# Two blocks of the first layer by turns, eight chunks ahead of them, and stores by block

## Chip, cores and metric

One core of one Trainium2 chip runs the whole program. The metric is device time in microseconds (us), the median of several runs. A profile of one further execution gives the span from its first to its last instruction and what every engine did in it. Five engines work beside each other, each through its own queue in the order in which the program was written down: PE (TensorE, the matmuls), DVE (VectorE), ACT (ScalarE), POOL (GpSimd) and SP, which here only issues DMAs.

## What is computed

A linear attention with a decay per channel, and then two feed-forward layers over 3072 tokens:

```python
batch, n_heads, seq, head_dim = (4, 8, 768, 48)     # d_model 384
for t in range(S):
    state = alpha[:, :, t, :, None] * state + np.einsum('bhd,bhe->bhde', k[:, :, t], v[:, :, t])
    y[:, :, t] = np.einsum('bhd,bhde->bhe', q[:, :, t], state)
x = y as (3072, 384)
h = x @ w_in                    # 384 x 2048
x = (h * np.cos(h)) @ w_out     # 2048 x 384
g, val = x @ w_gate, x @ w_val  # 384 x 1536 each
out = (g / (1 + np.exp(-g)) * val) @ w_out2
```

The weights come as 64-bit floats. Inputs and outputs of the matmuls of the two layers are split into a high and a low part, so that a product takes three matmuls (high by high, low by high, high by low).

## The kernel before

**Chunks.** The attention is cut into 24 chunks: 6 blocks of time (128 steps each) by 4 batches. A chunk loads its q, k and decay table (`attn_load`, `qka`, 112 partitions by 2052 floats) and its v (128 by 576), and `attn` writes down its operations. DVE scans the decays (L392), takes reciprocals (L396) and scans again (L399). POOL multiplies q and k by the results (L393, L402). PE forms the scores (L409), DVE masks them into `sm` (L420, twice), PE transposes k (L431), forms the outputs of the four pairs of heads (L447 from the state, L451 from the scores) and the growth of the state (L439). ACT and DVE then copy the outputs into the high and low part `xh` and `xl` of the block (L467, L471): one instruction for the first three pairs and three for the last pair, whose 96 rows must be spread over partitions 96 to 127 of three columns. DVE adds to the state (L483), POOL fades it (L488). ACT squares two inputs for a range statistic (L494).

**Blocks and slots.** Four chunks make a block of 512 tokens. The first layer takes 16 slots for a block. In a slot (`first_slot`), PE computes 128 hidden channels (`hidden`, L514, nine matmuls of 512 columns into one bank), a chain of ACT and DVE computes h cos(h) (L560, L561, L564, L565, L568, all of which read the bank or `s`), ACT and POOL split it (L526, L527), and PE contracts it into the three sum banks (`contract`, L542 six matmuls, L548 three). Contractions run up to three slots behind (`LAG`). The sum banks are banks 0 to 2. The banks for the hidden channels go round: 6 and 7 in block 0, 5 to 7 from block 1, 3 to 7 in the last block. After a block `spill` scales the sums and stores them. The second layer has 12 slots for a block of 27 matmuls each.

**Weights.** A unit holds one slot's `w_in` and `w_out`. `decode` turns a unit from 64-bit floats into two 32-bit parts: ACT takes the low bits (L278), DVE the upper bits in two halves of 384 columns through bank 5 (L85, L89), POOL adds (L94), ACT and DVE write the high and low part (L295, L300). Units 0 and 1 are decoded among the first chunks, 2 and 3 next, and each other one four slots ahead of its slot in block 0. The later blocks use the same decoded weights. The second layer's 18 units are decoded in blocks 1 to 4 (`stash`, L314 to L323), kept in memory and loaded again (`recall`).

**Order.** `register` writes down all operations with a priority; `Plan.lay` lays them out by a list of costs and priorities, and the engines' queues get that order once and for all. Its first part, before the change: chunks 0 to 3; then block 0, slot by slot, with a decode in each of the first twelve and chunks 4 to 7 spread over the block; then block 1 with chunks 8 to 11, and so on. The planner's numbers set the order alone; at run time each instruction waits for its semaphores.

**The end.** `ending` runs the last contractions bank by bank. A bank's halves are copied by ACT (L646) and DVE (L647), both into one buffer, and stored. `put` (L625) stores a block's result as 128 partitions by 4 batches by 128 columns.

## Time and profile before

| | |
|---|---|
| runs | 1024.91, 1025.81, 1027.52 us; median 1025.81 |
| profiled execution | 1021.61 us, its span 1019.8 us |
| PE busy | 988.0 us (97% of the span) |
| DVE, ACT, POOL busy | 524.8, 506.6, 418.4 us |
| first 150 us: PE, DVE busy | 125.5, 136.2 us |
| 150 to 450 us: PE, DVE busy | 300.0, 234.4 us |

A busy PE is not a PE at its peak, since the ends of matmuls are modelled and neighbours overlap. What it got done in a stretch is read better from the count of its instructions. A matmul of 32-bit attention operands counts as two instructions.

### The profile page before, as it was taken

The numbers are of one execution on the slowest core, as the hardware profiler recorded it, in microseconds if no ns is written. First come the engines' busy times: TensorE is split into PE (matmuls) and PEld (weight loads), VectorE is DVE, ScalarE is ACT, GpSimd is POOL, SyncE is SP. The second block draws the span as 40 slices with busy tenths as digits, with TensorE's granted clock in tenths as the row PEclk, the third lists the DMA queues.
The fourth block names the chain that finished last, engine by engine and source line by source line (L and its number), as shares of the span: only waits on it lengthen the run. The fifth ranks groups of instructions, "written<-read, shape, count | busy, mean of one in ns | idle before, by whom it ended". The sixth has DMA issues, their size and how long they took to land.

```text
span 1019.8 us, 12904 instructions
## 1 busy us (share of the span) xinstructions
PE 988.0 (97%) x4902; PEld 810.3 (79%) x4902; DVE 524.8 (51%) x785; ACT 506.6 (50%) x924; POOL 418.4 (41%) x323
## 2 busy tenths in 40 slices
PE   7689899999999999999999999999999999999997
PEld 7567678888888888888888888888888888888885
DVE  7999997887786788674433222322222222222221
ACT  3487676777777778776767223312212212221211
POOL 5666764555555458453434223223223223222221
PEclk9799999999999999999999999999999999999999
DMA  9456436434463654554576413201101100100101
GB/s 297 147 148 184 143 80 192 123 119 141 136 196 106 178 168 136 151 183 149 187 254 230 171 36 123 91 0 32 31 1 31 31 1 1 31 1 1 31 1 34
DMA packets 33685, 109.54 MB, mean 107 GB/s; under 512 B 2960, under 2 KB 12304, under 8 KB 31440
## 3 DMA queue, kind: packets, MB, share of 16 engines
q1 hardware_dynamic: 33616, 108.64, 35.0%
q8 instruction: 40, 0.66, 0.3%
q14 instruction: 29, 0.24, 0.1%
HBM read 85.04 MB, written 23.59 MB: 107 GB/s over the span
## 4 chain that ended last, share of the span: by engine, by line
PE 90%; DVE 7%; DMA 1%; issue 1%; ACT 1%; POOL 0%; DVEq 0%; SPq 0%
PE bank L514 47%; PE bank L542 22%; PE bank L548 11%; PE bank L451 4%; PE bank L409 2%; PE bank L447 2%; PE bank L439 1%; DMA qka<-qka 1%; DVE bank L85 1%; DVE ws L89 1%; DVE qka L399 1%; PE bank L431 1%; DVE pair L300 1%; DVE xl L471 1%; DVE s L568 1%
## 5 line engine op out<-in xcount | busy, mean ns | idle before, releaser
L527 POOL TENSOR_TENSOR glo<-s,ghi 128x512 fp32r<-128x512 f32 x168 | 233.9, 1392 | 483.3 <-ACT ghi L526 447.4
L514 PE MATMUL bank<-xh,late 128*128 128x512 f32 x864 | 282.3, 394 | 0.0
L514 PE MATMUL bank<-xh,pair 128*128 128x512 f32 x576 | 198.8, 400 | 9.1 <-DVE s L568 6.8
L578 DVE TENSOR_TENSOR s<-s,bank 128x512 f32<-128x512 f32 x72 | 49.5, 687 | 281.4 <-ACT s L577 281.4
L514 PEld LDWEIGHTS bank<-xh,late 128*128 128x128 f32 x864 | 162.7, 188 | 37.8
L526 ACT CAST ghi<-s 128x512 fp32r<-128x512 f32 x168 | 103.8, 618 | 160.4 <-DVE s L579 141.1
L514 PE MATMUL bank<-xl,late 128*128 128x512 f32 x432 | 170.1, 394 | 0.0
L542 PE MATMUL bank<-ghi,pair 128*128 128x512 f32 x576 | 151.4, 398 | 0.0
L577 ACT ACTIVATE s<-bank 128x512 f32<-128x512 f32 x72 | 43.1, 598 | 194.0 <-PE bank L514 193.8
L514 PEld LDWEIGHTS bank<-xh,pair 128*128 128x128 f32 x576 | 108.7, 189 | 37.6 <-DVE s L568 9.2
L542 PEld LDWEIGHTS bank<-ghi,pair 128*128 128x128 f32 x576 | 106.9, 188 | 24.9
L514 PE MATMUL bank<-xl,pair 128*128 128x512 f32 x288 | 114.2, 397 | 1.6 <-DVE xl L471 1.6
L542 PE MATMUL bank<-ghi,late 128*128 128x512 f32 x432 | 112.2, 395 | 0.0
L514 PEld LDWEIGHTS bank<-xl,late 128*128 128x128 f32 x432 | 81.4, 188 | 18.9
L542 PEld LDWEIGHTS bank<-ghi,late 128*128 128x128 f32 x432 | 81.3, 188 | 19.0
L561 DVE SCALAR_TENSOR_TENSOR s<-s,bank 128x512 f32<-128x512 f32 x96 | 65.4, 682 | 56.4 <-ACT s L560 55.7
L560 ACT ACTIVATE s<-bank,magic 128x512 f32<-128x512 f32 x96 | 66.0, 688 | 57.2 <-PE bank L514 55.5
L568 DVE SCALAR_TENSOR_TENSOR s<-s,bank 128x512 f32<-128x512 f32 x96 | 65.0, 677 | 45.6 <-ACT s L565 45.2
L548 PE MATMUL bank<-glo,pair 128*128 128x512 f32 x288 | 83.8, 399 | 0.1
L94 POOL TENSOR_TENSOR ws<-ws 128x768 int32<-128x768 int32 x34 | 66.9, 1966 | 40.1 <-DVE ws L89 32.6
L564 ACT ACTIVATE s<-s 128x512 f32<-128x512 f32 x96 | 60.5, 631 | 28.7 <-DVE s L561 28.4
L579 DVE TENSOR_TENSOR s<-s,bank 128x512 f32<-128x512 f32 x72 | 49.5, 687 | 48.3 <-PE bank L514 48.2
(96 smaller groups left out, 1202.7 us busy)
## 6 DMA issues: line engine op xcount, KB each, us to landing
big<-w SPq DMA_DIRECT2D x34, 768.0 KB, 5.5
qka<-qka SPq DMA_DIRECT2D x36, 384.8 KB, 6.3
w2d<-big SPq DMA_DIRECT2D x18, 768.0 KB, 4.1
late<-w2d SPq DMA_DIRECT2D x18, 768.0 KB, 4.3
ws<-w SPq DMA_DIRECT2D x16, 768.0 KB, 4.6
v<-vv SPq DMA_DIRECT2D x22, 288.0 KB, 3.0
x2d<-big SPq DMA_DIRECT2D x6, 768.0 KB, 3.8
big<-x2d SPq DMA_DIRECT2D x6, 768.0 KB, 4.9
```

What stands on the lines that cost most here:

```text
L94: nc.gpsimd.tensor_tensor(a, a, low, ALU.add)
L514: nc.tensor.matmul(h, lhsT=self.part(key, wpart, c), rhs=act[:, c, :], start=(n == 0), stop=(n == 3 * KM - 1))
L526: self.add(ACT, 0.62, prio, lambda: nc.scalar.copy(hi, s), reads=[sc], writes=[hic])
L527: self.add(POOL, 1.29, prio, lambda: nc.gpsimd.tensor_sub(lo, s, hi.bitcast(F32)), reads=[sc, hic], writes=[loc], lock=True)
L542: nc.tensor.matmul(self.banks[m][0], lhsT=self.part(key, wpart, m), rhs=hi, start=(f == 0 and wpart == 0), stop=False)
L548: nc.tensor.matmul(self.banks[m][0], lhsT=self.part(key, 0, m), rhs=lo, start=False, stop=last)
L560: add(ACT, WIDE, p, lambda: nc.scalar.activation(s, h, AF.Identity, bias=self.magic), reads=[hc], writes=[sc])
L561: add(DVE, WIDE, p, lambda: nc.vector.scalar_tensor_tensor(s, s, MAGIC, h, ALU.subtract, ALU.subtract), reads=[hc], writes=[sc])
L564: nc.scalar.activation(s, s, AF.Sin, scale=HALF_TURN)
L568: add(DVE, WIDE, p, lambda: nc.vector.scalar_tensor_tensor(s, s, 0.5, h, ALU.subtract, ALU.mult), reads=[hc], writes=[sc])
L578: add(DVE, WIDE, p, lambda: nc.vector.tensor_tensor(s, s, hg, ALU.mult), reads=[gc], writes=[sc])
L579: add(DVE, WIDE, p, lambda: nc.vector.tensor_tensor(s, s, hv, ALU.mult), reads=[vc], writes=[sc])
```

## The change

The eight chunks of blocks 0 and 1 are written down first (`for ch in range(2 * B)`), with units 0 to 3 decoded among them. Then the slots of blocks 0 and 1 go by turns: slots 0 to 4 of block 0, then one slot of block 1 after every second slot of block 0, until block 0 is done; then block 1's other ten slots, with chunks 8 to 11 among them; then blocks 2 to 5 as before. Block 0 keeps its sums in banks 0 to 2, every other block has them in banks 3 to 5 (`LATE = 3`). The hidden banks are 6 and 7 until block 0 is done, then 2, 6 and 7, and 0, 1, 2, 6 and 7 from the last block.

In the first eight chunks (`PACKED = 8`) PE writes the last pair's outputs itself to partitions 96 to 127 (`thirds`), so that ACT and DVE each copy all outputs by one instruction. From unit 5 on (`QUICK = 5`) DVE decodes the upper bits in SBUF over all 768 columns at once (two instructions) in place of four halves through bank 5. Chunks 0 to 3 load their inputs in four pieces. Their first state is a product on DVE alone, without POOL's fade. Chunks 4 to 7 take the four input buffers in turn, as 0 to 3 did. The second layer's units are decoded from position 33 on. The result is stored block by block, contiguous in the columns of a block (the host puts the columns in order), and in the ending DVE copies its half of the last bank into a buffer of its own. Most of the planner's costs and priorities have new numbers.

```diff
+PACKED = 8
+QUICK = 5
+LATE = 3
+JOIN = 4
+PACE = 2
+STASH = 33
...
+        if i < QUICK:
+            bits, bc = self.banks[5]
...
+        else:
+            add(DVE, 0.55, prio, lambda: decode_quick(nc, high, a), reads=[rc], writes=[ac], lock=True)
+            add(DVE, 0.95, prio, lambda: decode_sign(nc, high, a, a), reads=[rc], writes=[ac], lock=True)
...
+        if ch < PIECES:
+            for n, p in zip("FRqk", PARTS):
+                self.add(SP, 0.45, prio + p, lambda n=n: piece(n), writes=[cells[n]], lat=0.75)
...
-        base = 0 if ch < FAST and ch % 2 else 3
+        base = 3 if ch < 2 * B and ch % 2 == 0 else 0
...
+        def thirds():
+
+            for j in range(3):
+                part = slice(32 * j, 32 * j + 32)
+                uses = [
+                    (v[:, 3, i : i + 2, :].rearrange("s a e -> s (a e)")[:, part], self.sm[i][0][:, 3, :])
+                    for i in range(2) if j != 2 - 2 * i
+                ]
+                if not first:
+                    uses.insert(0, (st[0:ROWS, 3].rearrange("p a e -> p (a e)")[:, part], q[:, 3, :]))
+                for n, (w, x) in enumerate(uses):
+                    nc.tensor.matmul(o[96:128, j, :], lhsT=w, rhs=x, start=(n == 0), stop=(n == len(uses) - 1))
...
+        if packed:
+            outs = [(o[:, 0:3, :], (slice(0, 128), slice(0, 3), cs))]
...
+                    if first:
+                        nc.vector.tensor_tensor(s, u, fend[lo:hi].unsqueeze(2).to_broadcast([hi - lo, PAIRS, D]), ALU.mult)
...
-            src, c = self.banks[m]
+            src, c = self.banks[y + m]
...
-            outv[:, m, :, blk * C : (blk + 1) * C], ob[:, m, :].rearrange("p (b t) -> p b t", b=B)
+            self.out[m * 128 : (m + 1) * 128, blk * N + cols.start : blk * N + cols.stop], src
...
+            add(ACT, 0.4, prio, lambda m=m, src=src: nc.scalar.copy(ob[:, m, left], src[:, left]), reads=[bc], writes=[own])
+            add(DVE, 0.4, prio, lambda src=src: nc.vector.tensor_copy(other[:, left], src[:, right]), reads=[bc], writes=[oc])
...
+        for ch in range(2 * B):
+            self.attn_load(ch, LOADS[ch])
+            if ch in (1, 2, 3, 4):
+                self.decode(ch - 1, DEC[ch - 1], DLOAD[ch - 1])
+            self.attn(ch, FIRST[ch])
+        order, n1 = [], 0
+        for f in range(F1):
+            order.append((0, f))
+            if f >= JOIN and (f - JOIN) % PACE == 0:
+                order.append((1, n1))
+                n1 += 1
+        order += [(1, f) for f in range(n1, F1)] + [(blk, f) for blk in range(2, NB) for f in range(F1)]
```

PE's queue in the middle of block 0, before. `xh_62` and `xl_63` are block 0's input, banks 104 and 105 are hidden banks 6 and 7, banks 98 to 100 are block 0's sums, and `qka` and `st_88` belong to chunk 4, whose parts stand between the slots:

```order
L514 MATMUL bank_104<-xh_62,pair 128x512
L542 MATMUL bank_98<-ghi_69,pair 128x512 x2
L542 MATMUL bank_99<-ghi_69,pair 128x512 x2
L542 MATMUL bank_100<-ghi_69,pair 128x512 x2
L548 MATMUL bank_98<-glo_73,pair 128x512
L548 MATMUL bank_99<-glo_73,pair 128x512
L548 MATMUL bank_100<-glo_73,pair 128x512
L431 MATMUL bank_101<-ident,qka 128x112 x4
L542 MATMUL bank_98<-ghi_70,pair 128x512 x2
L542 MATMUL bank_99<-ghi_70,pair 128x512 x2
L542 MATMUL bank_100<-ghi_70,pair 128x512 x2
L447 MATMUL bank_102<-qka,st_88 96x128
```

The same engine now, in the middle of block 0 after all eight chunks. `xh_64` and `xl_65` are block 1's input, banks 101 to 103 its sums:

```order
L611 MATMUL bank_99<-glo_73,pair 128x512
L611 MATMUL bank_100<-glo_73,pair 128x512
L576 MATMUL bank_104<-xh_64,pair 128x512
L576 MATMUL bank_104<-xl_65,pair 128x512
L576 MATMUL bank_104<-xh_64,pair 128x512 x2
L576 MATMUL bank_104<-xl_65,pair 128x512
L576 MATMUL bank_104<-xh_64,pair 128x512 x2
L576 MATMUL bank_104<-xl_65,pair 128x512
L576 MATMUL bank_104<-xh_64,pair 128x512
L604 MATMUL bank_101<-ghi_70,pair 128x512 x2
L604 MATMUL bank_102<-ghi_70,pair 128x512 x2
L604 MATMUL bank_103<-ghi_70,pair 128x512 x2
```

No part of a chunk stands between slots there any more; a slot of block 1 takes the place, by weights that are decoded already.

DVE's queue in block 0, before. Two steps of a slot's chain (L561, L568) hold four halves of a decode between them; `big` is the raw unit, bank 103 is bank 5:

```order
L561 SCALAR_TENSOR_TENSOR s_66<-s_66,bank_105 128x512
L85 TENSOR_SCALAR bank_103<-big_77 128x384
L89 SCALAR_TENSOR_TENSOR ws<-big_77,bank_103 128x384
L85 TENSOR_SCALAR bank_103<-big_77 128x384
L89 SCALAR_TENSOR_TENSOR ws<-big_77,bank_103 128x384
L568 SCALAR_TENSOR_TENSOR s_66<-s_66,bank_105 128x512
L561 SCALAR_TENSOR_TENSOR s_67<-s_67,bank_104 128x512
L85 TENSOR_SCALAR bank_103<-big_78 128x384
L89 SCALAR_TENSOR_TENSOR ws<-big_78,bank_103 128x384
L85 TENSOR_SCALAR bank_103<-big_78 128x384
L89 SCALAR_TENSOR_TENSOR ws<-big_78,bank_103 128x384
L568 SCALAR_TENSOR_TENSOR s_67<-s_67,bank_104 128x512
```

The same engine now, in the part where blocks 0 and 1 go by turns (L627 and L634 are the chain's steps, L103, L107 and L325 the decode's):

```order
L627 SCALAR_TENSOR_TENSOR s_67<-s_67,bank_105 128x512
L103 TENSOR_SCALAR ws<-big_78 128x768
L107 SCALAR_TENSOR_TENSOR ws<-big_78,ws 128x768
L325 TENSOR_TENSOR pair<-ws,pair 128x768
L634 SCALAR_TENSOR_TENSOR s_67<-s_67,bank_105 128x512
L627 SCALAR_TENSOR_TENSOR s_68<-s_68,bank_104 128x512
L103 TENSOR_SCALAR ws<-big_77 128x768
L107 SCALAR_TENSOR_TENSOR ws<-big_77,ws 128x768
L634 SCALAR_TENSOR_TENSOR s_68<-s_68,bank_104 128x512
L627 SCALAR_TENSOR_TENSOR s_66<-s_66,bank_105 128x512
L325 TENSOR_TENSOR pair<-ws,pair 128x768
L634 SCALAR_TENSOR_TENSOR s_66<-s_66,bank_105 128x512
```

A decode's upper bits are two instructions there, both from SBUF to SBUF, and of three slots in a row one has no decode of upper bits in its chain.

## Rows read from the trace of the kernel before

**Rows 1.** Stretches: from:to, length, busy us (count) of each engine, PEclk, DMA.

```profile
0.00:150.00 150.00, 125.49 (x768) 105.29 (x769) 136.18 (x215) 97.43 (x188) 95.07 (x82) 0.94 0.58 168
6.00:49.00 43.00, 29.32 (x223) 26.88 (x222) 39.99 (x61) 18.59 (x47) 24.80 (x20) 0.84 0.76 237
49.00:150.00 101.00, 91.55 (x527) 73.77 (x526) 95.52 (x150) 77.36 (x139) 66.46 (x48) 0.98 0.50 137
150.00:450.00 300.00, 300.00 (x1679) 248.64 (x1678) 234.43 (x333) 221.96 (x417) 171.06 (x126) 1.00 0.52 151
600.00:1000.00 400.00, 400.00 (x1725) 324.27 (x1724) 95.70 (x146) 96.73 (x164) 97.33 (x76) 1.00 0.09 28
```

**Rows 2.** Stretches, PE and PEld alone: L514 (two rows), then L542, then L548.

```profile
0.00:150.00 150.00, 41.04 (x153) 28.35 (x153) 0.94 0.58 168
150.00:450.00 300.00, 127.24 (x504) 94.07 (x504) 1.00 0.52 151
...
0.00:150.00 150.00, 20.96 (x80) 14.99 (x81) 0.94 0.58 168
...
0.00:150.00 150.00, 11.41 (x39) 7.13 (x39) 0.94 0.58 168
```

**Rows 3.** Waits of PE, 45 to 120 us: in total, times, longest.

```profile
PE bank L514 <- DVE s L568: 6.0, 5, 2.7
```

**Rows 4.** Timeline, DVE's first scan: start, us, operation, idle before it.

```profile
6.37 1.23 DVE L392 TENSOR_TENSOR_SCAN qka<-qka,starts 112x516 f32<-112x516 f32 x1 [4.81 <-DMA qka<-qka]
```

**Rows 5.** DVE's groups by line, 6 to 49 us: count, busy us, mean ns, idle before.

```profile
L399 DVE TENSOR_TENSOR_SCAN qka<-qka,rb 112x512 f32<-112x512 f32 x3 | 5.9, 1958 | 0.1
L471 DVE SCALAR_TENSOR_TENSOR xl<-bank,xh 32x128 fp32r<-32x128 f32 (+1 forms) x16 | 5.6, 351 | 1.0 <-ACT xh L467 0.8
L420 DVE COPY_PREDICATED sm<-mask,bank 128x512 f32<-128x512 int32 x8 | 5.4, 726 | 0.3 <-PE bank L409 0.2
L392 DVE TENSOR_TENSOR_SCAN qka<-qka,starts 112x516 f32<-112x516 f32 x3 | 4.4, 1463 | 5.4 <-DMA qka<-qka 5.3
...
L85 DVE TENSOR_SCALAR bank<-big 128x384 int32<-128x384 int32 x6 | 3.3, 558 | 0.1
L89 DVE SCALAR_TENSOR_TENSOR ws<-big,bank 128x384 int32<-128x384 int32 x6 | 3.3, 553 | 0.2
...
L483 DVE TENSOR_TENSOR st<-st,bank 48x192 f32<-48x192 f32 x8 | 2.8, 352 | 0.2
L300 DVE TENSOR_TENSOR pair<-ws,pair 128x768 fp32r<-128x768 f32 x2 | 2.1, 1074 | 0.0
L396 DVE RECIPROCAL rb<-qka 112x32 f32<-112x32 f32 x3 | 1.0, 349 | 0.0
```

**Rows 6.** Groups by line and form, whole span: count, busy us, mean ns, idle before.

```profile
L561 DVE SCALAR_TENSOR_TENSOR s<-s,bank 128x512 f32<-128x512 f32 x96 | 65.4, 682 | 56.4 <-ACT s L560 55.7
...
L89 DVE SCALAR_TENSOR_TENSOR ws<-big,ws 128x768 int32<-128x768 int32 x18 | 21.9, 1218 | 0.4
...
L471 DVE SCALAR_TENSOR_TENSOR xl<-bank,xh 96x384 fp32r<-96x384 f32 x24 | 13.2, 550 | 6.2 <-ACT xh L467 5.9
...
L85 DVE TENSOR_SCALAR ws<-ws 128x768 int32<-128x768 int32 x18 | 12.1, 671 | 0.5
```

**Rows 7.** Timeline, DVE and POOL in blocks 1 and later, single instructions.

```profile
182.76 1.85 POOL L94 TENSOR_TENSOR ws<-ws 128x768 int32<-128x768 int32 x1 [0.96 <-DVE ws L89]
183.14 1.89 DVE L316 TENSOR_SCALAR ws<-ws 128x768 f32<-128x768 f32 x1
185.06 0.56 DVE L85 TENSOR_SCALAR ws<-ws 128x768 int32<-128x768 int32 x1
186.73 0.95 DVE L89 SCALAR_TENSOR_TENSOR ws<-big,ws 128x768 int32<-128x768 int32 x1
...
993.11 1.29 POOL L527 TENSOR_TENSOR glo<-s,ghi 128x512 fp32r<-128x512 f32 x1 [4.99 <-ACT ghi L526]
```

**Rows 8.** Timeline, the last copy ahead of the last store.

```profile
1013.01 0.42 DVE L647 COPY big<-bank 128x256 f32<-128x256 f32 x1 [1.30 <-ACT big L646]
```

More of the change, by code (lines that the diff above doesn't have):

```diff
@@ L105 @@
 class Op:
-    __slots__ = ("engine", "cost", "emit", "need", "prio", "lock", "lat", "users", "left", "ready", "start", "end", "number", "heirs")
+    __slots__ = ("engine", "cost", "emit", "need", "prio", "lock", "lat", "users", "left", "ready", "start", "end", "number", "heirs", "span")
 class Plan:
@@ L172, in lay @@
             op.start = max(t, other) if op.lock else t
-            free[e] = op.start + op.cost
+            free[e] = op.start + op.span
             if op.lock and e in port:
@@ L475, in attn @@
         hc = Cell()
-        add(ACT, 1.25, prio, high, reads=[sc1c], writes=[hc], joins=[xc])
-        add(DVE, 1.42, prio, low, reads=[sc1c, hc], joins=[xc])
+        add(ACT, 0.5 if packed else 1.25, prio, high, reads=[sc1c], writes=[hc], joins=[xc])
+        add(DVE, 0.55 if packed else 1.42, prio, low, reads=[sc1c, hc], joins=[xc])
         if not last:
@@ new lines, in register @@
+        units = list(range(F1, W2))
+        held = ring(6, 7)
+        chunks = list(range(2 * B, NCH))
+        for g, (blk, f) in enumerate(order):
+            if blk == 0 and f + 4 < F1:
+                self.decode(f + 4, g + LEAD, g - 6)
+            if 0 in self.spilled and g >= STASH and (g - STASH) % 3 == 0 and units:
+                self.stash(units.pop(0), g)
+            if blk == NB - 1:
+                if f == 0:
+                    held = ring(0, 1, 2, 6, 7)
+                if f < 2:
+                    self.recall(F1 + f, g)
+                if f > LAG:
+                    self.recall(F1 + 2 + f - LAG - 1, g)
+                if f == F1 - 2:
+                    self.load(0, g)
+            s = self.first_slot(blk, f, held, g)
+            y = LATE if blk else 0
+            queue.append((("out", f), y, s, F1, (lambda p, blk=blk, y=y: self.spill(blk, p, y)) if f == F1 - 1 else None))
+            flush(LAG if (blk, f) != (0, F1 - 1) else 0, g + 0.5)
+            if (blk, f) == (0, F1 - 1):
+                held = ring(2, 6, 7)
+                left = len([0 for b, _ in order[g + 1 :] if b < 2])
+                self.xt[2] = self.xs.next()
+                for j in range(B):
+                    start = g + 1 + SPREAD * j
+                    self.attn_load(2 * B + j, start - 5)
+                    self.attn(2 * B + j, start)
+            if blk >= 2 and blk + 1 < NB and f % 4 == 0:
+                ch = B * (blk + 1) + f // 4
+                if f == 0:
+                    self.xt[blk + 1] = self.xs.next()
+                start = g + GAP * (f // 4) - f - AHEAD
+                self.attn_load(ch, start - 5)
+                self.attn(ch, start)
```

217 lines of the change are left out of this document (114 added, 103 removed).

## Prediction

> **What bounds the kernel now.** The stretches come first [rows 1]. From 150 us on PE is busy without a gap, 300.00 of 300 us and later 400.00 of 400. In the first 150 us it is busy 125.49, and DVE 136.18: there DVE sets the pace, 39.99 of 43 us in the first chunks and 95.52 of 101 in block 0. The reader should turn this into work done. In the second layer PE passes 1725 instructions in 400 us, 0.232 us each; this is the price of a matmul of 512 columns at full rate. In 150 to 450 us 504 of them are hidden channels [rows 2], and the contractions are as many, 1008 together or 234 us. The other 671 instructions of that stretch are attention, and for them 66 us are left, 0.099 us each. By these prices the first 150 us hold 153 + 80 + 39 = 272 big matmuls [rows 2], 63.1 us, and 768 - 272 - 60 = 436 attention instructions [rows 1] (60 are the warm-up loop), 43.2 us. So 106.3 us of work were done in 150 us, and **43.7 us are lost to PE**, all of them there. Nothing the change does later can give much. The waits name the chain as well: six of the lost microseconds are a hidden bank that waits for the last DVE step of an earlier slot [rows 3].
>
> **The first eight chunks.** The change does the eight chunks before most of block 0, so the question is when DVE is through with them. Per chunk before [rows 5]: first scan 1.46, reciprocal 0.35, second scan 1.96, masks 5.4 / 4 = 1.35, low half 5.6 / 4 = 1.40, state 2.8 / 4 = 0.70. The packed outputs put one instruction of 0.55 [rows 6] in place of 1.40, so a chunk is 1.46 + 0.35 + 1.96 + 1.35 + 0.55 + 0.70 = 6.37, eight of them 51.0 us. In DVE's order five decodes through the bank stand ahead of the last chunk's end, (3.3 + 3.3) / 3 = 2.2 each, 11.0; five low parts of weights at 1.05, 5.3 [rows 5]; five chain steps at 0.68, 3.4, and three SBUF decode steps, 0.67 + 1.22 + 0.67 = 2.6 [rows 6]. Together 73.3 us of busy time. Before, DVE was busy 39.99 of the 42.6 us from its first scan to 49 us [rows 1, 4], 94%. At the same density 73.3 becomes 78.1 us.
>
> It starts earlier. Before, the first scan waits until 6.37 us for the whole table, 4.81 of it idle [rows 4]; now its own quarter comes first. If the idle time went with the bytes, it would begin 3.6 earlier, at 2.8; with no gain at 6.4. I take 4.2, between the two. The end is then 4.2 + 78.1 = 82 us. PE is through with the last chunk some 2 us before that (what follows is an ACT copy, the low half and the state): 80 us.
>
> By then PE has done 4 chunks of 44 attention instructions and 4 of 52, 384 x 0.099 = 38.0 us (the extra matmuls of the packed outputs not counted), and the hidden channels of three slots, 27 x 0.232 = 6.3. That is 44.3 us of work in 80, **35.7 lost** against 43.7: a gain of 8.0 us. The packed outputs add 2 matmuls in each of the first four chunks and 4 in the next, 48 instructions or 4.8 us at full rate. They cost nothing as long as DVE is the late one, since PE is busy only 29.32 of 43 us there [rows 1]; without that cover they would cost their 4.8. The clock granted there is 0.84 on average, between its two levels of 1.2 and 2.4 GHz; since PE will be as idle, I expect the same, and it is in the density. POOL's four fades that go were not waited for.
>
> **Blocks 0 and 1 by turns.** From 80 us PE has work without chunks: from the fourth slot to the last of block 0 there are 18 slots, 18 x 18 x 0.232 = 75 us. A new unit is needed every 1.5 slots instead of every slot, and no chunk stands between. Three slots are 12.5 us of PE, and DVE then has six chain steps, 4.1 us, and two decodes of 0.67 + 1.22 + 1.05 [rows 5, 6], 5.9: 10.0 of 12.5, 80%. That is near the 234.43 of 300 at which PE never waits, and below the 95.52 of 101 at which it does [rows 1]. But only two hidden banks are there, as in block 0 before, against three later. So the loss lies between nothing (the row from 150 us) and block 0's own idle share, 9.45 us in 91.55, which on 75 us is 7.7. I take 4. Ahead of block 2 the last of chunks 8 to 11 must be ready with only some 3.5 us of other work for PE behind it; its DVE steps fit by their rows to within a microsecond, which I leave in the 4.
>
> The decode through the bank cost 2.2 us and had PSUM on one side of every step. The new form costs 0.56 + 0.95 = 1.51 alone [rows 7], but it can be held. DVE's L316 began 0.38 us after a POOL addition of 1.85, took 1.89 and ended 0.42 us behind POOL's end; L85 next to it, of the same size and without POOL beside it, took 0.56 [rows 7]. The halves through the bank take 0.56 and 0.55 in the mean [rows 5], so none is held. The Trainium skill, GPSIMD Engine Reference, section Key points, states this as a rule: POOL's SBUF interfaces are shared with VectorE, which meets contention in a two-port mode or with two SBUF inputs. By that rule 11 decodes move 16.6 us of DVE time into the shared kind, while by DVE's length alone they save 11 x 0.7 = 7.6 us; the sum above has the held means, and the rule's own result is the second rival.
>
> **The end and the rest.** The last DVE copy, 0.42 us, comes behind ACT's before [rows 8] and now runs beside it; the two smaller stores are issued one behind the other, so between -0.5 and 1; I take 0.5. Stores by block, later decodes of the second layer and the new bank numbers lie beside a PE that is busy without a gap: nothing, unless a late weight is waited for, which no row there shows.
>
> **Sum.** 8.0 - 4 + 0.5 = 4.5 us less than the profiled 1021.6 (span 1019.8), which lies 4.2 below the median of the runs. I put the difference on the median: 1025.8 - 4.5 = **1021.3 us**.
>
> **Rivals.**
>
> *A, the start waits for its loads.* Ahead of the last chunk's first scan, eight inputs of 112 x 2052 and 128 x 576 floats and four units of 786 kB must come, 12.9 MB. At the 237 GB/s of the first chunks [rows 1] that is 54 us, and by the sum above DVE wants it at 55. For it: no slack at that rate. Against: that rate is a mean with pauses. A tenth less costs 5 us: 1021.3 + 5 = 1026, no change.
>
> *B, DVE and POOL hold each other while the blocks go by turns.* If their SBUF operations exclude each other, three slots need 2 x (0.56 + 0.95 + 0.95) of DVE and 2 x 1.85 + 3 x 1.29 of POOL [rows 7] (a low part of weights is the size of the 0.95), 12.5 us of PE's 12.5. DVE's queue would be the place: its own 4.1 + 4.9 = 9.0 us leave 3.5 for six waits, so from 0.6 us of wait for each PE is held. At 1.2, a little below a whole POOL operation, three slots take 9.0 + 7.2 = 16.2 us, 3.7 more, and 11 units are 5.5 such turns: 20 us in place of 4, 1021.3 + 16 = 1037; at 0.9, 10 us: 1027. The turns eat the whole gain of 8.5 from a wait of 0.84 (9.0 + 6 x 0.84 = 14.05, 1.55 over, 5.5 times), and this is the point from which the kernel is slower than before. For it: the pair of rows above. Against: the mean of L89, 1.22, shows a wait of 0.27 [rows 6], and POOL may run behind by a slot. The rule named above would bring it about, and the trace agrees that the hold exists.
>
> *C, the start goes better.* If the packed chunks come at DVE's length alone (73.3 us, no idle time), 4.8 us more, and the turns cost nothing, 4 more: 1012.5.
>
> *D, the plan's order brings nothing because block 1 begins late.* The order shows its slots from the sixth position on, so I give it no chance of its own.
>
> **How the numbers follow.** My forecast has 0.60, A 0.13, B 0.17, C 0.10. What a measurement of this kernel can tell from no change is about 0.3%, 3 us. The forecast's own spread, 1014 to 1028 by its bounds (start 2 either way, density 3, turns 4), puts 0.42 of its 0.60 below 1022.7 and 0.15 within; C is all below, A mostly within, B mostly above. Faster 0.54, same 0.28, slower 0.18. The range must leave out no more than 0.2: from 1011 (a little under C) to 1031 (B's milder half).
>
> **What would show it.** In the trace after: DVE's first scan near 4 us; the last output of the eighth chunk on PE near 80 us; DVE near 94% until then; a low half of 0.55 us once per chunk; afterwards PE's waits for L634 no more than 4 us in all until block 0 is done, and DVE near 80% there. If PE's waits there are over 10 us and L103, L107 and L325 take over 1.5 us in the mean, B is right; if DVE's scans wait for loads by more than 4 us, A. A last chunk later than 88 us would sink the forecast whatever follows.

## The result, and the profile after

The changed kernel takes **1010.62 us** (median; 1009.87 to 1011.95) against 1025.36 (1023.03 to 1027.52) for the kernel before beside it: a ratio of 0.9858, 95% interval 0.9834 to 0.9882. In a second measurement (below) it took 1012.05 against 1022.83, 0.9885 (0.9867 to 0.9904). So 11 to 15 us went, where 4.5 were forecast; the first measurement lies just under the forecast's range. The profiled executions, 1010.5 and 1021.6 us, have spans of 1008.4 and 1019.8: 11.4 us are there to be found. Which execution is profiled is chance: those of the changed kernel were 1010.5 and, in the second measurement, 1013.6 us.

The stretches of the kernel after (from:to, length, busy us and count of each engine, PEclk, DMA), to be held against [rows 1]:

```profile
0.00:150.00 150.00, 137.03 (x829) 115.67 (x830) 127.62 (x169) 94.05 (x169) 92.70 (x75) 0.97 0.58 168
6.00:49.00 43.00, 33.50 (x268) 29.16 (x267) 35.32 (x49) 16.28 (x37) 18.64 (x15) 0.88 0.93 262
3.60:77.70 74.10, 62.50 (x511) 55.03 (x509) 65.15 (x94) 35.04 (x75) 37.91 (x32) 0.93 0.84 228
77.70:153.00 75.30, 75.30 (x326) 60.84 (x325) 64.23 (x73) 59.49 (x97) 54.44 (x34) 1.00 0.31 105
150.00:450.00 300.00, 300.00 (x1721) 249.75 (x1720) 229.15 (x332) 218.42 (x417) 162.09 (x125) 1.00 0.48 139
```

Nearly all that was won was won in the first 150 us, PE 125.49 to 137.03. The fourth row is the surprise: while the blocks go by turns PE never waits. Its waits of the first 150 us (total, times, longest) are all from the chunks, but for the 1.4 us ahead of its first work, and the wait for DVE's last step of a hidden channel, 6.0 us before [rows 3], is gone:

```profile
PE bank L465 <- DVE sm L454: 9.0, 4, 4.9
PE bank L373 <- POOL ident masks.py:199: 1.4, 1, 1.4
PE bank L443 <- issue: 1.0, 2, 0.8
PE bank L576 <- ACT xh L520: 0.8, 1, 0.8
PE bank L473 <- ACT kt L469: 0.7, 1, 0.7
```

The timeline gives the two ends of the start, DVE's first scan (6.37 before, [rows 4]) and the last chunk's state on PE, and below them the end of the program:

```profile
3.64 1.23 DVE L426 TENSOR_TENSOR_SCAN qka<-qka,starts 112x516 f32<-112x516 f32 x1 [2.09 <-DMA qka<-qka]
...
77.02 0.94 PE L473 MATMUL bank<-both,kt 128*112 128x96 f32 x8
...
1002.85 0.37 ACT L721 COPY big<-bank 128x256 f32<-128x256 f32 x1 [1.51 <-PE bank L611]
1003.33 0.42 DVE L722 COPY s<-bank 128x256 f32<-128x256 f32 x1 [8.15 <-ACT big L721]
1003.78 1.58 SPq L690 DMA_DIRECT2D out<-s  x1
```

Six of DVE's 17 groups in the start, 3.6 to 77.7 us (count, busy us, mean ns, idle before), as [rows 5]:

```profile
L433 DVE TENSOR_TENSOR_SCAN qka<-qka,rb 112x512 f32<-112x512 f32 x4 | 6.6, 1644 | 0.2
L433 DVE TENSOR_TENSOR_SCAN spare<-spare,rb 112x512 f32<-112x512 f32 x4 | 6.5, 1617 | 0.2
L426 DVE TENSOR_TENSOR_SCAN tails<-tails,starts 112x516 f32<-112x516 f32 x4 | 5.9, 1496 | 0.0
L103 DVE TENSOR_SCALAR bank<-big 128x384 int32<-128x384 int32 x10 | 5.5, 554 | 1.9 <-DMA big<-w 1.8
L426 DVE TENSOR_TENSOR_SCAN qka<-qka,starts 112x516 f32<-112x516 f32 x4 | 4.9, 1228 | 5.7 <-DMA qka<-qka 5.7
L524 DVE SCALAR_TENSOR_TENSOR xl<-bank,xh 128x384 fp32r<-128x384 f32 x7 | 3.8, 549 | 1.5 <-ACT xh L520 1.5
```

And the groups of DVE and POOL that work from SBUF to SBUF in the turns, 77.7 to 153 us:

```profile
L107 DVE SCALAR_TENSOR_TENSOR ws<-big,ws 128x768 int32<-128x768 int32 x10 | 17.2, 1719 | 0.2
L325 DVE TENSOR_TENSOR pair<-ws,pair 128x768 fp32r<-128x768 f32 x11 | 13.0, 1179 | 0.0
L103 DVE TENSOR_SCALAR ws<-big 128x768 int32<-128x768 int32 x10 | 8.6, 858 | 0.0
...
L589 POOL TENSOR_TENSOR glo<-s,ghi 128x512 fp32r<-128x512 f32 x18 | 28.6, 1591 | 16.8 <-ACT ghi L588 9.1 <-issue 4.1 <-PE bank L611 2.5
L112 POOL TENSOR_TENSOR ws<-ws 128x768 int32<-128x768 int32 x11 | 23.4, 2131 | 7.2 <-DVE ws L107 5.4 <-PE bank L576 1.8
```

Against their lengths alone, 0.95, 0.95 and 0.56 [rows 7], DVE's three wait 0.77, 0.23 and 0.30 us, 0.43 in the mean. The timeline shows one of these waits: L107 begins under a POOL subtraction, takes 1.94 in place of 0.95, and ends 0.82 us behind POOL's end.

```profile
98.24 1.71 POOL L589 TENSOR_TENSOR glo<-s,ghi 128x512 fp32r<-128x512 f32 x1 [0.25 <-POOL ws L112]
98.83 1.94 DVE L107 SCALAR_TENSOR_TENSOR ws<-big,ws 128x768 int32<-128x768 int32 x1
```

**Where the 11.4 us are.** Counted as the prediction counted: 829 instructions to 150 us, of them 60 of the warm-up and 337 big ones, leave 432 of attention, and 48 of these are the extra ones of the packed outputs (the view counts 180, 106 and 51 of L576, L604 and L611). So 337 x 0.232 + 384 x 0.099 = 78.2 + 38.0 = 116.2 us of the old work are done, 33.8 lost where it was 43.7: **9.9 us**. The end takes 4.65 us from the last copy's end (1003.75) to the span's, before 6.4 (1013.43 to 1019.8): **1.7**. That is 11.6 of 11.4. The medians of the first measurement differ by 14.7: the execution of before that was profiled, 1021.6 us, was a quick one, and that of the changed kernel lay at its median.

### The profile page after: what moved, and what is told of

It reads as the page before. It is cut to its first block, busy times and chain, and to the rows that moved or that the text cites. A ratio compares the mean times of both kernels' runs of the same rounds, so it can differ in the third digit from the quotient of the medians.

```text
span 1008.4 us, 12954 instructions
## 1 busy us (share of the span) xinstructions
PE 989.8 (98%) x4950; PEld 813.1 (81%) x4950; DVE 517.5 (51%) x737; ACT 498.8 (49%) x900; POOL 407.3 (40%) x315
## 4 chain that ended last, share of the span: by engine, by line
PE 95%; DMA 3%; DVE 1%; issue 0%; ACT 0%; SPq 0%; DVEq 0%; ACTq 0%
PE bank L576 50%; PE bank L604 23%; PE bank L611 12%; PE bank L501 3%; PE bank L443 2%; PE bank L497 2%; PE bank L473 1%; DMA big<-w 1%; DMA v<-vv 1%; PE bank L490 1%; PE bank L465 1%; DMA spare<-qka 1%; DMA qka<-qka 1%; DVE spare L433 0%; DVE sm L454 0%
## 5 line engine op out<-in xcount | busy, mean ns | idle before, releaser
L589 POOL TENSOR_TENSOR glo<-s,ghi 128x512 fp32r<-128x512 f32 x168 | 230.5, 1373 | 468.0 <-ACT ghi L588 414.4
L576 PE MATMUL bank<-xh,late 128*128 128x512 f32 x864 | 282.3, 394 | 0.0
L576 PE MATMUL bank<-xh,pair 128*128 128x512 f32 x576 | 196.0, 397 | 0.8 <-ACT xh L520 0.8
L576 PEld LDWEIGHTS bank<-xh,late 128*128 128x128 f32 x864 | 162.7, 188 | 37.8
L588 ACT CAST ghi<-s 128x512 fp32r<-128x512 f32 x168 | 103.6, 618 | 160.5 <-DVE s L645 147.0
L576 PE MATMUL bank<-xl,late 128*128 128x512 f32 x432 | 170.1, 394 | 0.0
L604 PE MATMUL bank<-ghi,pair 128*128 128x512 f32 x576 | 151.0, 397 | 0.0
L576 PEld LDWEIGHTS bank<-xh,pair 128*128 128x128 f32 x576 | 108.3, 188 | 27.2 <-ACT xh L520 1.0
L604 PEld LDWEIGHTS bank<-ghi,pair 128*128 128x128 f32 x576 | 107.2, 188 | 25.0
L576 PE MATMUL bank<-xl,pair 128*128 128x512 f32 x288 | 113.9, 395 | 0.1
L604 PE MATMUL bank<-ghi,late 128*128 128x512 f32 x432 | 112.2, 395 | 0.0
L576 PEld LDWEIGHTS bank<-xl,late 128*128 128x128 f32 x432 | 81.4, 188 | 18.9
L604 PEld LDWEIGHTS bank<-ghi,late 128*128 128x128 f32 x432 | 81.3, 188 | 19.0
L627 DVE SCALAR_TENSOR_TENSOR s<-s,bank 128x512 f32<-128x512 f32 x96 | 65.7, 684 | 49.6 <-ACT s L626 49.0
L634 DVE SCALAR_TENSOR_TENSOR s<-s,bank 128x512 f32<-128x512 f32 x96 | 65.2, 680 | 42.3 <-ACT s L631 41.7
L611 PE MATMUL bank<-glo,pair 128*128 128x512 f32 x288 | 83.4, 398 | 0.0
```

Of the source, the lines that this page charges most:

```text
L576: nc.tensor.matmul(h, lhsT=self.part(key, wpart, c), rhs=act[:, c, :], start=(n == 0), stop=(n == 3 * KM - 1))
L588: self.add(ACT, 0.62, prio, lambda: nc.scalar.copy(hi, s), reads=[sc], writes=[hic])
L589: self.add(POOL, 1.29, prio, lambda: nc.gpsimd.tensor_sub(lo, s, hi.bitcast(F32)), reads=[sc, hic], writes=[loc], lock=True)
L604: nc.tensor.matmul(self.banks[y + m][0], lhsT=self.part(key, wpart, m), rhs=hi, start=(f == 0 and wpart == 0), stop=False,)
L611: nc.tensor.matmul(self.banks[y + m][0], lhsT=self.part(key, 0, m), rhs=lo, start=False, stop=last)
L627: add(DVE, WIDE, p, lambda: nc.vector.scalar_tensor_tensor(s, s, MAGIC, h, ALU.subtract, ALU.subtract), reads=[hc], writes=[sc])
```

## The experiments

The theory after the result: DVE and POOL hold each other on SBUF, as rival B had it, and the turns, by asking for fewer weight units per slot, keep that hold below what PE would feel; the start gains by DVE's shorter work. The rivals: the chain from a hidden bank to the low part, or DVE's own length, holds PE where there are no turns; and loads, or a chain over several engines, carry the start. Each kernel was timed beside the kernel before. A ratio is to that kernel in the same set, and 0.001 is 1.0 us. The changed kernel's own ratios are the 0.9858 and 0.9885 above.

### How far runs lie apart

The kernel before and the changed one, each run again without an edit.

> The kernel before, unchanged, in further executions. The medians differ by 14.7 us, the two profiled spans (1019.8 and 1008.4) only by 11.4. Theory 1, the profiled execution before was a quick one: its spans scatter over 1019 to 1026 us, and the difference between a short and a long one lies in the first 150 us, where PE waits for others; the typical loss there is then 46 to 48 us, not 43.7. Theory 2, the 3 us lie outside the span or in the profiling: spans all within 1 us of 1020.

> The changed kernel without an edit, as the yardstick for the others of this set and for how far its runs lie apart. Theory 1: its start scatters as that of the kernel before does (the last chunk's output at 77 to 81 us), spans of 1008 to 1012 us and a median of 1010 to 1013 us. Rival: the first measurement stands for all, 1010 to 1011 us with the last chunk's output within half a microsecond of 77.0.

Before: 1023.63 us (1022.31 to 1027.12), ratio 1.0004 (0.9985 to 1.0023). After: 1012.05 (1010.23 to 1013.63). Both kernels scatter, before by 5 to 7 us and after by 2 to 3.5, but after was run only four times in each set. The first theory of either expectation fits, but for the size of the typical loss in before. In the second profile of before, of span 1021.4, the first 150 us lose 45.3 us by the prices of the prediction, where 43.7 were lost in the first: that is all of the 1.6 us between their spans. In after it is the start as well, 3.5 us more lost in the first 150 at a span 3.1 longer. The row of the last chunk's state in the second profile, of span 1011.5, is 2.3 us later than in the first:

```profile
79.27 0.94 PE L473 MATMUL bank<-both,kt 128*112 128x96 f32 x8
```

So a difference of 2 us between two variants says little here.

### The parts: turns and packed outputs

No turns at all, then turns from slot 13 of block 0 on; packed outputs taken out of the changed kernel, and put alone into the kernel before.

```diff
-JOIN = 4
+JOIN = 16        # then: 13
```

```diff
-PACKED = 8
+PACKED = 0
```

> The changed kernel with block 0 alone after the eight chunks and block 1 behind it. Per slot PE has 4.18 us. Theory 1, DVE and POOL exclude each other on SBUF: a slot with its decode needs 0.56 + 0.95 + 0.95 of DVE and 1.85 + 1.29 of POOL, 5.6 us, 1.4 too much, over 11 slots 10 to 15 us: 1020 to 1026 us, with waits of PE for L634 or L325. Theory 2, the turns are not needed: DVE alone has 1.36 + 2.46 = 3.8 us per slot, so 0 to 3 us: 1010 to 1014.

> The changed kernel with the turns beginning at slot 13 of block 0 in place of slot 4 (so one or two slots of block 1 are taken in before block 0 ends, where it was six); all else as in the changed kernel. If the turns are what frees TensorE after the chunks (theory 1), nearly the whole gain over the kernel before goes: 1021 to 1025 us, with named waits of TensorE of 7 us or more between 80 and 150 us, and its busy time in 77.7 to 153 us near 67.7 of 75.3 us, as where no turn is left. Rival: the gain comes from the eight chunks first and the packed outputs, and the turns only move work about: 1011 to 1014 us.

> The changed kernel with the outputs of the first eight chunks copied in four pieces as before. DVE gets 0.85 us more per chunk, 6.8 in eight, and PE 48 instructions less. Theory 1, DVE's length sets when the eight chunks are through: 5 to 7 us longer, 1016 to 1018. Theory 2, the loads set it (DVE waited about 5 us for them in the profile): 0 to 3 us longer, 1011 to 1014.

> The kernel before with the packed outputs in its first eight chunks and nothing else. DVE loses 6.8 us of work in the first 150 us, where it was busy 136. Theory 1, DVE's length sets the time there: 5 to 7 us shorter, 1018 to 1020. Theory 2, in block 0 it is the chain of one slot, held up by the order of the queues, and PE has 2 to 4 more matmuls per chunk without a gap to hide them: 0 to 3 us shorter, 1022 to 1025.

(In the two with fewer turns, and below in the one with two quarters first and the one with half of a subtraction, one weight unit of the second layer is overwritten before it is stored, since the range test's buffers share its place and are not tied to it in the plan. The instructions and their number are those of the full work.)

No turns: 1024.25 us, 0.9993 (0.9973 to 1.0014). Turns from slot 13: 1026.39, 1.0021 (1.0001 to 1.0041). **Without the turns nothing is left of the gain**; they are worth 12 to 16 us. Unpacked: 1018.84, 0.9952 (0.9931 to 0.9973), so the packing is worth 7 to 10 us inside the changed kernel. Packed alone: 1020.07, 0.9964 (0.9947 to 0.9981), some 3 us of the kernel before. No turns falls into theory 1's range, unpacked lies a little over theory 1's, and packed alone between its two theories. So the two parts do not add: with packing and no turns nothing is left, with the turns and no packing 4 to 5 us. The edits of the turns and of the packing also make the plan write another order, so a part's price holds its order too.

With turns from slot 13, the stretch of the turns reads (same columns as above, then DVE's groups):

```profile
77.70:153.00 75.30, 69.58 (x290) 53.39 (x289) 70.17 (x71) 54.31 (x87) 57.20 (x32) 0.98 0.30 105
...
L325 DVE TENSOR_TENSOR pair<-ws,pair 128x768 fp32r<-128x768 f32 x11 | 16.0, 1458 | 0.0
L107 DVE SCALAR_TENSOR_TENSOR ws<-big,ws 128x768 int32<-128x768 int32 x11 | 15.6, 1421 | 0.1
L103 DVE TENSOR_SCALAR ws<-big 128x768 int32<-128x768 int32 x10 | 12.2, 1220 | 0.0
L627 DVE SCALAR_TENSOR_TENSOR s<-s,bank 128x512 f32<-128x512 f32 x14 | 9.5, 679 | 3.9 <-ACT s L626 3.7
```

DVE is busy 70.17 of 75.30 and gets through 14 slots where after it is 18. The reader should work it out per slot: two chain steps, 2 x 0.68 = 1.36; a unit's three operations, 0.56 + 0.95 + 0.95 = 2.46; and their waits here, 0.66 + 0.47 + 0.51 = 1.64. That is 5.46 us of DVE for 4.18 of PE, and 11 units are decoded in this way: by this sum 11 x 1.28 = 14.1 us would be lost. With the turns three slots share two units: 6 x 0.68 + 2 x 2.46 + 6 x 0.43 = 11.6 of 12.5, nothing lost.

The trace gives less than that sum. In this stretch PE passed 276 big matmuls where after it passed 323, and 14 attention instructions where after it passed 3; by the prices of the prediction 9.9 us were lost there, against 0.1. Of the 16.2 us between the two spans some 10 thus lie in this stretch, 1 ahead of it and the rest behind it, from 153 to 450 us, where PE again waits for L634 and for the masks of later chunks. The waits that the expectation asked for, 7 us or more, came to 5.5:

```profile
PE bank L604 <- ACT ghi L588: 3.1, 3, 1.4
PE bank L611 <- POOL glo L589: 1.3, 2, 0.7
PE bank L576 <- DVE s L634: 0.9, 1, 0.9
PE bank L576 <- DVE pair L325: 0.2, 1, 0.2
```

The rest is slower matmuls, part of it by the clock: behind PE's waits of 0.31, 0.74 and 1.37 us the granted clock fell to 0.50, its lower level, and six matmuls that had taken 1.67 us at 106.58 took 2.93.

```profile
111.31 2.93 PE L604 MATMUL bank<-ghi,pair 128*128 128x512 f32 x6 [1.37 <-ACT ghi L588]
...
112.00:114.00 2.00, 2.00 (x6) 1.56 (x5) 2.00 (x3) 1.31 (x2) 2.00 (x2) 0.50 0.00 0
```

### Is it the hold, or the chain's length?

Three edits on the decode and on POOL: a second subtraction on POOL in each slot of blocks 0 and 1; turns from slot 13 with all units decoded through the bank; turns from slot 13 with POOL's subtraction on half of its columns.

```diff
+            for _ in range(2 if twice else 1):
+                nc.gpsimd.tensor_sub(lo, s, hi.bitcast(F32))
```

```diff
-JOIN = 4
-QUICK = 5
+JOIN = 13
+QUICK = 16        # and the range test's buffers tied to the stash
```

```diff
-nc.gpsimd.tensor_sub(lo, s, hi.bitcast(F32))
+nc.gpsimd.tensor_sub(lo[:, 0:w], s[:, 0:w], hi.bitcast(F32)[:, 0:w])    # w = 256, JOIN = 13
```

> The changed kernel with one more GpSimd subtraction (1.29 us alone, the same operands again) in each of the 32 slots of blocks 0 and 1; the order of instructions is otherwise as in the changed kernel. Theory 1: while the blocks go by turns VectorE and GpSimd do exclude each other on SBUF, and the room they have is nearly used up (single lengths of their SBUF operations fill about the whole 75 us). Then 3 slots ask for 12.5 + 3 x 1.29 = 16.4 us in place of 12.5, VectorE's operations wait longer and TensorE with them: 18 slots of block 0 with 11 of block 1 are some 6 such threes until 153 us, so +15 to +23 us over the changed kernel (1026 to 1034), with TensorE waiting for VectorE's chain steps (L634) or weights after 80 us. Theory 2: the hold is a wait of some tenths that GpSimd's own length sets, not a shared capacity; GpSimd was busy 54.4 of 75.3 us there and has room for another 18 x 1.29 = 23 us: +0 to +2 us, and TensorE without a wait after 80 us.

> The changed kernel with the turns beginning at slot 13 (as in the run that began them there, 1026.4 us) and all sixteen units of the first layer decoded through the PSUM bank, in halves, as before (in that run eleven were decoded in SBUF). Per slot of block 0 VectorE then has 2 x 0.68 for the chain, 2.2 + 0.95 for the unit: 4.5 us, 0.7 more than with the decode in SBUF, against 4.18 us of TensorE; but the SBUF operations that VectorE and GpSimd can't do at once are 0.95 + 1.85 + 1.29 = 4.1 us in place of 2.46 + 3.14 = 5.6. Theory 1 (the engines exclude each other on SBUF, and that is what holds TensorE where no turns thin the units out): the time falls by 6 to 12 us against 1026.4, to 1014 to 1020. Rival (VectorE's own length or the chain holds it): 14 slots lose another 0.3 us each or more, 1028 to 1033 us.

> The kernel with the turns beginning at slot 13 (1026.4 us), with GpSimd's subtraction of 1.29 us working on half of its columns in blocks 0 and 1 from the fifth slot on (some 0.65 us less each; outputs differ for that reason, and one weight unit of the second layer is overwritten, as in the run it is compared with). GpSimd was busy 57 of 75 us there, so its own length binds nothing. Theory 1: VectorE's port operations wait out GpSimd's, and that fills VectorE (70 of 75 us busy, L103, L107 and L325 at 1.17 to 1.47 us in place of 0.56 to 0.95): the holds get shorter, and the time falls by 4 to 9 us, to 1017 to 1022. Rival: the length of the chain from hidden bank to low part holds TensorE (its waits for the low part were 1.3 us in all): at most 1.5 us less, 1025 to 1027.

**Second subtraction:** 1026.83 us, 1.0027 (1.0010 to 1.0044), some 15 us slower than after, the time of theory 1. But the view of the stretch shows POOL full, so it was not DVE alone that held PE:

```profile
77.70:153.00 75.30, 68.93 (x279) 53.13 (x278) 66.00 (x62) 53.04 (x82) 74.05 (x43) 0.97 0.28 100
...
L592 POOL TENSOR_TENSOR glo<-s,ghi 128x512 fp32r<-128x512 f32 x30 | 51.9, 1737 | 1.3
```

The subtraction takes 1.74 in place of 1.29: POOL is held by DVE as well, 30 x 0.45 = 13 us. What the rival's expectation said of room on POOL was worked out wrongly, since 54.4 + 18 x 1.29 is already 77.6 us; the run shows the hold on POOL's side, and does not by itself tell the theories apart.

**Through the bank:** 1024.62, 1.0011 (0.9999 to 1.0023), 2 us less than its pair; neither theory's time. The one operation of DVE that is still from SBUF to SBUF waits longer than each of the three did (the profiled execution, 1027.88 us, was the slowest of its ten):

```profile
77.70:153.00 75.30, 66.32 (x284) 51.02 (x283) 73.41 (x95) 56.31 (x89) 54.02 (x32) 1.00 0.31 105
...
L325 DVE TENSOR_TENSOR pair<-ws,pair 128x768 fp32r<-128x768 f32 x11 | 23.2, 2113 | 0.0
```

L325 waits 1.16 us each time. DVE's slot is then 1.36 + 2.2 + 0.95 + 1.16 = 5.67 us, about the 5.46 of the SBUF form. So theory 1 was put in the wrong quantity: the sum of both engines' SBUF operations fell and the time hardly did. DVE's own queue, its lengths and its waits, agrees better: DVE is busy 73.41 of 75.30 us there. Fewer such operations waited longer each.

**Half subtraction:** 1021.87, 0.9979 (0.9963 to 0.9994), 4.5 us less than its pair, where the rival allowed 1.5:

```profile
77.70:153.00 75.30, 69.59 (x292) 53.86 (x290) 62.81 (x72) 55.86 (x87) 50.41 (x33) 1.00 0.29 99
...
L107 DVE SCALAR_TENSOR_TENSOR ws<-big,ws 128x768 int32<-128x768 int32 x11 | 14.5, 1322 | 0.1
L325 DVE TENSOR_TENSOR pair<-ws,pair 128x768 fp32r<-128x768 f32 x11 | 14.0, 1272 | 0.0
L634 DVE SCALAR_TENSOR_TENSOR s<-s,bank 128x512 f32<-128x512 f32 x16 | 10.9, 680 | 4.0 <-ACT s L631 3.9
L103 DVE TENSOR_SCALAR ws<-big 128x768 int32<-128x768 int32 x9 | 8.2, 909 | 0.0
```

All three waits fall, to 0.35, 0.37 and 0.32, and 16 slots pass. By the same sum a slot is 1.36 + 2.46 + 1.04 = 4.86, 11 x 0.68 = 7.5 us lost in place of 14.1: 6.6 less by the sum, 4.5 by the medians. The order of the instructions is the same. So it is shown that DVE's operations wait out POOL's, and that less work on POOL makes the program faster, though POOL was not full. How much of the 4.5 us comes by DVE's waits is not shown, since the edit also shortens the chain to the low part: PE's waits for L589 fell from 1.3 to 0.2 us, and the clock, 0.98 in the stretch of its pair, stayed at 1.00. Nor is the hold the only cause: DVE has 12 us of idle time in this run, and PE still waits 2.8 us for ACT's L588 and 0.8 for L634 in the stretch, which is the chain with two hidden banks.

The sum on DVE's queue, against what PE lost from 77.7 to 153 us by the prices of the prediction:

| kernel | by the sum, us | lost, us |
|---|---|---|
| after | 0 | 0.1 |
| turns from slot 13 | 14.1 | 9.9 |
| the same, through the bank | 16.4 | 11.3 |
| the same, half subtraction | 7.5 | 7.6 |

The sum puts the runs in their order and not at their size. A run without turns whose units are decoded ahead of block 0 would part the decodes from the chain; it was not made.

### What carries the start

Six edits: the first four chunks' tables loaded whole; their first two quarters ahead of everything; 2.4 MB of loads less; half of DVE's masks and second scans in chunks 4 to 7; the first values one place later; and with that, all units decoded in SBUF.

```diff
-PIECES = 4
+PIECES = 0
```

```diff
-PARTS = (-3, -1, 0, 1)
+PARTS = (-40, -39.5, 0, 1)
```

```diff
-nc.sync.dma_start(raw, self.w[i])
+nc.sync.dma_start(raw[0:rows], self.w[i][0:rows])      # 8 rows for units 2 and 3; no q columns for chunks 4 to 7
```

```diff
-nc.vector.tensor_tensor_scan(R, R, rb, 0.0, ALU.mult, ALU.add)
+nc.vector.tensor_tensor_scan(R[:, 0:w], R[:, 0:w], rb[:, 0:w], 0.0, ALU.mult, ALU.add)    # and the masks
```

```diff
-self.add(SP, 0.45, prio + 5, lambda: nc.sync.dma_start(v, self.v[ch])
+self.add(SP, 0.45, prio + (17.5 if ch == 0 else 5), lambda: nc.sync.dma_start(v, self.v[ch])
```

```diff
-QUICK = 5
+QUICK = 0         # with the edit above, and the range test's buffers tied to the stash
```

> The changed kernel with the tables of the first four chunks loaded whole, as before, in place of in quarters; nothing else is changed. Theory 1: VectorE's first scan waits until about 6.4 us in place of 3.6, and VectorE carries the start: the last chunk's output 2 to 3 us later, 1012 to 1014 us. Rival: the bytes are the same and the loads carry the start, so only the first scan moves: 0 to +1 us, 1010 to 1012.

> The changed kernel with the first two quarters of the tables of chunks 0 to 3 asked for ahead of everything else, so that VectorE's scans of these chunks have their inputs early; nothing else is changed. Theory 1: VectorE's waits for transfers in the start (2.98 us ahead of the second scan, 1.77 and 0.59 later) sit on the path, since VectorE carries the start: -2 to -4 us against the changed kernel (1007 to 1009). Rival: the weights and inputs come late by the bytes that stand ahead of them, whatever their order, and the time is lost later in the start: -1 to +1 us.

> The changed kernel with 2.4 MB fewer loaded in the start, all instructions of the engines and their order kept: chunks 4 to 7 don't load their queries (they use what the chunk four before left there), and weight units 2 and 3 load 8 of 128 partitions (the rest is the unit that lay there before). Outputs differ for that reason. At the 262 GB/s of 6 to 49 us these bytes are 9.1 us. Theory 1: the loads carry the start (the transfer engines are 93% busy in 6 to 49 us, and VectorE waits 7 us for them): the last chunk's output comes 4 to 9 us earlier than 77, and the time falls by 4 to 8 us, to 1003 to 1007. Rival: VectorE's own length carries it (65 of 74 us busy): at most 2 us less, 1009 to 1011.

> The changed kernel with less work on VectorE in chunks 4 to 7, all instructions and their order kept: the masks and the second scan work on half of their columns (outputs differ for that reason). Eight masks at 0.73 and four scans at 1.62 fall to about half, some 5 us in all. Theory 1: VectorE carries the start from 20 us on (it is busy 46.5 of 50 us in 20 to 70): -3 to -5 us against the changed kernel, 1007 to 1009, and the last chunk's output that much earlier. Rival: a chain of waits over the engines carries it and VectorE's time only fills it: 0 to -1 us.

> The changed kernel with the second chunk's first quarter asked for ahead of the first chunk's values, in SyncE's queue one place earlier; nothing else is changed, and the result is the same. VectorE's second scan waited 2.98 us for that quarter. 0.295 MB less stand ahead of it, 1.1 us at 270 GB/s. Theory 1 (VectorE carries the start): -0.5 to -1.2 us, 1009 to 1011. Rival: the first chunk's values come later by as much, and the first chunk's outputs on TensorE with them: 0 to +1.

> As the run before it in this set, and the first five units too decoded in SBUF in place of through the bank in halves, so that nothing but its own length and the holds differs: VectorE's own length falls by 5 x 0.7 = 3.5 us in the start. GpSimd is busy there 38 of 74 us. Theory 1: the holds take part of it back (half of GpSimd's time, a mean wait of some 0.3 us for ten operations, 3 us): -1 to +1 us against that run. Rival: VectorE's length alone counts: -3 to -4 us, 1006 to 1008.

| edit | us | ratio (95%) | last chunk's state on PE in the profiled execution, us |
|---|---|---|---|
| whole tables | 1017.22 | 0.9943 (0.9923 to 0.9963) | 80.14 |
| two quarters first | 1023.18 | 0.9991 (0.9973 to 1.0009) | 91.85 |
| 2.4 MB less | 1011.98 | 0.9894 (0.9877 to 0.9912) | 76.44 |
| half of DVE's masks, scans | 1010.46 | 0.9866 (0.9841 to 0.9891) | 77.00 |
| first values later | 1014.31 | 0.9911 (0.9889 to 0.9933) | 78.82 |
| and all units in SBUF | 1016.34 | 0.9926 (0.9903 to 0.9949) | 85.03 |

The two that take work away move nothing that can be told from the scatter: neither the later loads nor DVE's own length carries the start alone, and both theories that said so fell. With 5 us less on DVE the time went into waits there, 3.1 us for PE and 3.1 for a weight, which after were at most 1.8. The four that move or merge the first loads, or change the decodes, all cost: 2 us, at the edge of the scatter, to 12, though the bytes are the same. Neither theory gave the time of any of the four, and none of them is a test of the loads alone, whatever its expectation says: from the new priorities the plan wrote another **order** for DVE, POOL and ACT as well. With the first values later, for one, DVE does the second chunk's second scan behind the first scans of chunks 2 and 3, at 16.45 us in place of 11.26. The largest miss was the two quarters first: chunk 0's other quarters and the first weight then come behind 1.4 MB more (two quarters of three chunks, 0.23 MB each), and in DVE's queue the first decode now stands ahead of the first masks. The waits of DVE and of PE name the loads, and the masks, first after and then in this run, the order:

```profile
DVE bank L103 <- DMA big<-w: 6.2, 1, 6.2
...
PE bank L443 <- POOL qka L436: 6.5, 2, 5.9
...
12.40 1.32 DVE L454 COPY_PREDICATED sm<-mask,bank 128x512 f32<-128x512 int32 x2
...
23.27 1.35 DVE L454 COPY_PREDICATED sm<-mask,bank 128x512 f32<-128x512 int32 x2
```

Whole tables cost 5 us, where the first scan began 2.6 us later (6.22), twice what was expected. What remains open is which single chain through the start is the longest, and what of these costs is the loads' and what the order's. The packing took 6.8 us of work from DVE and three of four copies of each chunk from ACT, and was worth 7 to 10 us; 5 us less on DVE in chunks 4 to 7 gave nothing. Which of the two engines counted in the packing was not tried. None of these orders beat the changed kernel's.

### The end

The outputs laid out as before, rows of 512 bytes in place of 1 and 2 KB.

```diff
-            self.out[m * 128 : (m + 1) * 128, blk * N + cols.start : blk * N + cols.stop], src
+            outv[:, m, b0:b1, blk * C : (blk + 1) * C], src.rearrange("p (b t) -> p b t", t=C)
```

> The changed kernel with the outputs laid out as before (rows of 512 bytes in DRAM in place of 1 and 2 KB runs). From VectorE's last copy to the end of the span passed 4.65 us after and 6.4 before. Theory 1: the shorter end is the layout's, whose last store goes in longer runs: +1.2 to +1.8 us, and 6 us or more from the last copy to the end. Rival: it is that the last two stores are half as large, the layout is nothing: 0 to +0.5 us, and 4.5 to 5 us there.

1012.87 us, 0.9880 (0.9846 to 0.9915): within the spread of the changed kernel. The last copy in the timeline, of a span of 1010.5:

```profile
1005.66 0.42 DVE L724 COPY s<-bank 128x256 f32<-128x256 f32 x1 [8.15 <-ACT big L723]
```

From its end, 1006.08, to the span's are 4.4 us, not more than with the new layout. So the shorter end is not the layout's. What else differs there is that the last bank goes out in two stores of half the size, DVE's from a buffer of its own; that was not tried by itself.

## Why the prediction was wrong, step by step

**Where the time is lost: right.** All but the end's 1.7 us of the gain lies in the first 150 us, and the later stretches are as full as before.

**The eight chunks: right in kind, 1.9 us short.** The last chunk's output was put at 80 us and came at 77.0 and 79.3 in two executions; the loss was put at 35.7 and is 33.8. The sum of DVE's groups was 73.3 and is 68.7 (all 17, of which six are shown). Most of the difference is the scans: 1.35 and 1.64 in the mean, where 1.46 and 1.96 were taken. Those were one group of two: the same view of before has the other chunks' scans at 1.72 and 1.52, and the means of all five are 1.57 and 1.78. Why the scans are shorter now was not tried. The first scan began at 3.64, forecast 4.2. The low half took 0.55, one per chunk, as said. The density did not hold: DVE was busy 65.15 of 74.10 us, 88%, where 94% was taken by the same measure, so a shorter sum at a lower density came out near the forecast, which is partly luck. The clock was 0.88, forecast 0.84. And the forecast let all of it rest on DVE's length, and the run with 5 us less on DVE says that this alone is not what sets it. Rival A's mark, over 4 us of waits of the scans for loads, was met: 5.7, of which 5.1 in the first 20 us. Yet as it was put, by the bytes ahead of the last chunk, A is out, since 2.4 MB less gave nothing and that chunk's first scan, at 55.03 us, waited for no load.

**The turns: wrong, and this is the step that failed.** A loss of 4 us was taken, half way between nothing and block 0's old idle share, because two hidden banks stand there as before. The trace after has none: PE is busy 75.30 of 75.30 us from 77.7 to 153, with the same two hidden banks, and DVE 64.23, 85%. In the second profile PE is busy 74.22 there, and its one wait, 1.1 us, is for a chunk's state (L540). The prediction's own arithmetic for rival B could have given it: PE is held from a wait of 0.6 us, the pairs of rows showed up to 1.3 and the mean of L89 0.27, and the measured mean is 0.43. Rival B's mechanism is real and below its point. The Trainium skill, GPSIMD Engine Reference, section Key points, has the rule that POOL shares its SBUF interfaces with VectorE; the waits above agree with it, in both directions, and it gives no size. The size is what decided, as far as the runs show: at one unit a slot, with waits of 0.55 in the mean, PE lost 9.9 us in this stretch and the program 12 to 16. What was not seen at all is that the turns are the condition of the gain and not its price: with the eight chunks first and no turns the kernel is as slow as before.

**The end: wrong in mechanism, a gain of 1.7 in place of 0.5.** DVE's copy does not run beside ACT's; it begins behind it (1003.33, ACT's 1002.85 + 0.37), as before [rows 8]. The gain comes after the copies.

**The sum and its base.** 9.9 + 0 + 1.7 stands where 8.0 - 4 + 0.5 stood: 7.1 us. From the profiled 1021.6 the measured terms lead to 1010.0, and 1010.5 was measured. The other 3.6 us of the miss are the base: the forecast put the difference on the median of before, 4.2 above its profiled execution, as if that distance stayed. Which execution was profiled is chance, and so is this part of the miss: after's lay at its median in the first measurement and 1.6 above it in the second. Of the cases listed, rival C (1012.5: the start goes better and the turns cost nothing) came nearest. It had a chance of 0.10; the row from 150 us on, where PE never waits with DVE 78% busy, spoke for it against the 80% forecast for the turns.

## What to carry to other kernels

Where two engines hold each other, work out the queue of the engine that is waited for per unit of the consumer's time, as own lengths plus waits: 11.6 of 12.5 us cost nothing here, and 16.4 of 12.5 cost 10 us in eleven slots where the sum says 14. Cutting the number of the operations moved it little, since the wait of the one that was left grew. A reordering that thins such work out can be the condition under which another edit pays, so price the edits together and each with the other undone. Compare a profiled execution with a profiled one, and don't carry the distance to the median over: it is the luck of one execution. And where a plan lays out the queues anew from priorities, compare the orders before an edit of one priority is read as a test of one load.

## What the runs showed that was not expected

POOL is held too: its subtraction of 1.29 alone took 1.59 in the mean beside the decodes, and 1.74 when doubled. The hold is not shared out by the number of operations: with one operation from SBUF to SBUF per unit left on DVE, that one waited 1.16 us, where three waited 0.55 each. And the start answers to its order, of loads and of instructions together, far more than to its bytes: 1.4 MB moved ahead, with the order that the plan then wrote, cost 12 us, and 2.4 MB left out later gave nothing.
